# Moving an uneven split from one weight load to a later one, a store to another queue, and regrouping the last stores

## The chip, the cores and the metric

One core of a Trainium2 chip runs the whole kernel. The metric is the device time in microseconds of one execution; several executions are timed and the median counts. All times inside the kernel are counted from the first instruction of the profiled execution.

## The reference

Pooled attention is followed by a soft mixture of experts. There are 8 batches, 8 heads, 576 positions and a head size of 64; the pool is 8; the experts are 8, with 4 slots each (32 slots), a hidden size of 1024 and a model size of 512.

```python
k_p = k.reshape(B, H, Sp, pool, D).mean(axis=3)
v_p = v.reshape(B, H, Sp, pool, D).mean(axis=3)
attn = softmax(scale * q @ k_p.T)               # 576 x 72 for each batch and head
x = (attn @ v_p) as [B * S, H * D]              # 4608 x 512
logits = x @ phi                                # 4608 x 32
slot_input = softmax(logits, axis=0).T @ x      # 32 x 512
for e in range(E):                              # 8 experts, 4 slots each
    slot_out[e] = relu(slot_input[e] @ w1[e]) @ w2[e]
out = softmax(logits, axis=1) @ slot_out        # 4608 x 512, float32
```

All inputs and the output are float32 in HBM. The kernel computes in bf16.

## The kernel before

**Loads.** Nearly everything is read by DMAs that POOL issues, which turn float32 into bf16 on the way. POOL's order is written by hand. It loads `q_sb`, `k_sb` and `v_sb` by pairs of batches (L71, 1152 KB each as bf16), then the eight `w1` matrices (`load_w1`, L78, tile `w_sb`, 1024 KB each), the `w2` of experts 0 to 3 into buffers of the attention (`w_big`, L86), those of experts 4 and 5 into the buffers of qT (`w_qT`, L86), and those of experts 6 and 7 into the buffers of xs (`load_last_w2`, tile `w_xs`, L94 to L98). This text writes w1[e] and w2[e] for the matrices of expert e. In a load of 128 partitions every partition reads one run of HBM: 16 KB for a whole w1 or w2 matrix (8 KB as bf16), 12 KB for the first six of eight rows of w2[6] at L94. At most eight transfers of POOL are in flight: each takes one of eight completion semaphores in turn and waits until the transfer before it on that semaphore has landed.

The load of w1[3] is cut by partitions into three transfers of 112, 8 and 8 partitions; all others have 128.

The last two matrices are loaded in pieces, in this order: w2[6] rows 0 to 5, both column parts (L94); then for each of the two parts of the columns (`PARTS`, 288 on the left and 224 on the right) w2[6] rows 6 and 7 (L96) and w2[7] rows 0 to 5 and 6 and 7 (L98).

**Compute.** Per pair of batches the kernel pools k and v by products with a constant matrix, transposes q, forms scores and exponentials, and the unnormalized `u`, normalizes it into `xs`, and sums up logits and slot inputs. After the last pair the experts' first products (`h_ps`, L432) and the second (`so_ps`, L476, `second`) follow. The order of the end is written out by hand: PE does `second` for experts 0 to 5, eight products on zeros (`warm(8, junk)`), the wide part of w2[6], six products on zeros (`warm(6, junk)`), then for the left and the right column part w2[7], the normalization `slots_out` (DVE, L480), and the output groups.

**Output.** A group of `GROUPS` with n tiles takes n x 128 rows of the output. For each tile PE forms a product `f_ps` (L494), and DVE (L498) or ACT (L496) evicts it by turns with a factor. The first four groups have two tiles and are done for the left and the right columns apart, into `o_sb`; the others have the whole width, into `w_sb`, which reuses the memory of w1. `output` issues the stores (L502) on SP, in the order of the groups; the very first group of each part is stored in two DMAs of 128 rows (`apart`), and in the left part the second group is stored by POOL. Before, the groups from the fifth on have 4, 4, 4, 8 and 8 tiles: three stores of 1 MB, then two of 2 MB.

Of the kernel before, what the change touches and what calls it, by code (L numbers as in the profile page):

```python
# [18 lines left out]
def kernel(  # L19
# [10 lines left out]
    nc = tc.nc  # L30
# [5 lines left out]
    E = moe_w1.shape[0]  # L36
# [11 lines left out]
    DJ = DM // 128  # L48
# [2 lines left out]
    HQ = H // 2  # L51
    NHALF = 4
    PARTS = [slice(0, 9 * DM // 16), slice(9 * DM // 16, DM)]
    GROUPS = [2] * NHALF + [4] * 3 + [8] * 2
    NSPLIT = 2
    NG = 128 // NS

# [15 lines left out]

    w1_sb = persist.tile([128, E, DJ, F], BF)

    def load_w1(e, cuts=()):
        for p0, p1 in zip((0,) + cuts, cuts + (128,)):
            nc.gpsimd.dma_start(out=w1_sb[p0:p1, e],  # L78
                                in_=moe_w1[e, p0 * DJ:p1 * DJ].rearrange("(p j) f -> p j f", j=DJ))

    w2_sb = [None] * E

    def load_w2(experts, pool, tag):
        for e in experts:
            w2_sb[e] = pool.tile([128, FJ, DM], BF, name=f"w2_{tag}", tag=tag)
            nc.gpsimd.dma_start(out=w2_sb[e], in_=moe_w2[e].rearrange("(p j) d -> p j d", j=FJ))  # L86

    def load_last_w2(pool, tag):

        j = FJ - NSPLIT  # L90
        src = [moe_w2[e].rearrange("(p j) d -> p j d", j=FJ) for e in range(E)]
        for e in (E - 2, E - 1):
            w2_sb[e] = pool.tile([128, FJ, DM], BF, name=f"w2_{tag}", tag=tag)
        nc.gpsimd.dma_start(out=w2_sb[E - 2][:, 0:j], in_=src[E - 2][:, 0:j])  # L94
        for cols in PARTS:
            nc.gpsimd.dma_start(out=w2_sb[E - 2][:, j:FJ, cols], in_=src[E - 2][:, j:FJ, cols])  # L96
            for j0, j1 in ((0, FJ - 2), (FJ - 2, FJ)):
                nc.gpsimd.dma_start(out=w2_sb[E - 1][:, j0:j1, cols], in_=src[E - 1][:, j0:j1, cols])  # L98
# [52 lines left out]
    for r in range(2):  # L151
        rows = slice(r * D, (r + 1) * D)
        nc.vector.tensor_copy(out=iphi[rows, :, 0:D],
                              in_=ident[rows, rows].rearrange("p d -> p () d").to_broadcast([D, H, D]))
# [9 lines left out]
    recC = persist.tile([128, 1], FP)  # L164
    recR = persist.tile([128, len(GROUPS), max(GROUPS)], FP)

# [6 lines left out]
    for pair in range(1, NP):  # L173
        for dst, src, name in ((k_sb, k, "k_sb"), (q_sb, q, "q_sb"), (v_sb, v, "v_sb")):
            dst[pair] = load_pair(src, pair, name)
        if pair == NP - 2:
            load_w1(0)

    for e in range(1, E):
        load_w1(e, cuts=(112, 120) if e == 3 else ())  # L180
    load_w2(range(4), big, "big")


# [171 lines left out]
    for pair in range(NP):  # L355
        for qd in range(2):
# [32 lines left out]
            if pair == NP - 1 and qd == 0:  # L389
                load_last_w2(xpool, "xs")  # L390
# [34 lines left out]
    for n in range(E // NG):  # L425
        for half in range(F // 512):
            cols = slice(half * 512, (half + 1) * 512)
            h_ps = ps_m.tile([128, 512], FP, name="h_ps", tag="m")
            for j in range(DJ):
                for g in range(NG):  # L430
                    e = n * NG + g
# [18 lines left out]
    groups = []  # L450
    for n in GROUPS:
        row0 = sum(128 * g[1] for g in groups)
# [4 lines left out]

    R_ps = ps_m.tile([128, len(groups), max(GROUPS)], FP, name="R_ps", tag="m")
    nc.vector.memset(R_ps, 1.0)
# [13 lines left out]
    def second(e, cols, rows=range(FJ)):  # L473
        for fj in rows:
            g = fj % NG
            nc.tensor.matmul(out=so_ps[g * NS:(g + 1) * NS, cols], lhsT=hT[:, e, fj], rhs=w2_sb[e][:, fj, cols],  # L476
                             start=(e == 0 and fj < NG), stop=(e == E - 1 and fj >= NG), skip_group_check=True)

    def slots_out(cols):
        nc.vector.tensor_scalar(out=so[:, cols], in0=so_ps[:, cols], scalar1=recC, scalar2=None, op0=ALU.mult)  # L480

    def output(g, cols, apart=False, queue=nc.sync):

        w = cols.stop - cols.start
        row0, n, rows = groups[g]
        if w == DM:

            e = (row0 // 128 - 2 * NHALF) // 4
            o_sb = w1_sb[:, e:e + n // 4].rearrange("p e j f -> p (e j f)").bitcast(FP).rearrange("p (r c) -> p r c", r=n)
        else:  # L490
            o_sb = opool.tile([128, n, w], FP, name=f"o_sb{w}", bufs=NHALF)
        for r in range(n):
            f_ps = ps_f.tile([128, w], FP, name="f_ps", tag="f")
            nc.tensor.matmul(out=f_ps, lhsT=rows(r), rhs=so[:, cols], start=True, stop=True)  # L494
            if r % 2:
                nc.scalar.activation(out=o_sb[:, r], in_=f_ps, func=AF.Copy, scale=recR[:, g, r:r + 1])  # L496
            else:
                nc.vector.tensor_scalar(out=o_sb[:, r], in0=f_ps, scalar1=recR[:, g, r:r + 1], scalar2=None,  # L498
                                        op0=ALU.mult)
        dst = out[row0:row0 + 128 * n].rearrange("(p r) c -> p r c", r=n)  # L500
        for rs in [slice(r, r + 1) for r in range(n)] if apart else [slice(0, n)]:
            queue.dma_start(out=dst[:, rs, cols], in_=o_sb[:, rs])  # L502


    junk = ps_m.tile([128, 512], FP, name="junk", tag="m")
# [6 lines left out]
    for c in range(2):  # L512
        second(E - 1, PARTS[c])
        slots_out(PARTS[c])
        for g in range(NHALF):

            output(g, PARTS[c], apart=g == 0, queue=nc.gpsimd if (c, g) == (0, 1) else nc.sync)
            if (c, g) == (0, 1):
                second(E - 2, PARTS[1], range(FJ - NSPLIT, FJ))
    for g in range(NHALF, len(groups)):  # L520
        output(g, slice(0, DM))
# [30 lines left out]
```

## Time and profile before

| | before |
|---|---|
| median of 4 runs | 176.53 us (176.51 to 176.63) |
| profiled execution, its own time | 176.63 us |
| its span, first to last instruction | 174.7 us |
| mean granted clock of TensorE | 0.876 |
| busy: PE, DVE, ACT, POOL | 131.5, 94.3, 82.7, 21.4 us |
| moved by POOL's queue (q0) | 30.12 MB, 84.1% of 16 engines' span |
| moved by SP's queue (q1) | 11.50 MB, 16.6% |

In the page's lines of 40 slices, each slice is 4.37 us; the DMA digits are tenths of the 16 DMA engines, and GB/s is what they moved, counted as bf16 where a transfer converts. The chain lists what released what, back from the last instruction: start in us, length in us, engine, tile and line. A line of the windows gives a stretch, its length, the busy time of each engine with the number of its instructions, the granted clock, the DMA share and the GB/s. A line of the timeline gives start and length of one instruction; SPq marks an issue on SP's queue. A line of the DMA issues gives tile and source, issuing queue, how many, the size of each as it is written, and the median time from issue to landing.

### The profile page before, as it was taken

What the parts mean: (1) busy time and instruction counts of PE and PEld (TensorE: products, weight loads), DVE (VectorE), ACT (ScalarE), POOL (GpSimd) and SP (SyncE); (2) the same over time, 40 slices, a digit from 0 to 9 for tenths busy, and PEclk for the clock granted to TensorE, in tenths of its full rate; (3) what the DMA queues carried; (4) which work ended last, traced back from release to release, by engine and by line L of the source; (5) the groups of instructions that cost most, each with busy time, mean ns of one, the idle gap of its engine ahead of it and who ended that gap; (6) DMA issues with size and microseconds to landing.
All of it is one profiled execution on the core that took longest, in us unless ns stands there. A gap on an engine that the chain in (4) does not pass through costs nothing.

```text
span 174.7 us, 3315 instructions
## 1 busy us (share of the span) xinstructions
PE 131.5 (75%) x1357; PEld 80.9 (46%) x1359; DVE 94.3 (54%) x257; ACT 82.7 (47%) x147; POOL 21.4 (12%) x42
## 2 busy tenths in 40 slices
PE   7505799999999999999999975999581198788000
PEld 2304667757866678665754443635440023322000
DVE  2306442677767888778786579543710002899000
ACT  3205459897946988657797540121100001799000
POOL 6000101121000610111130011112111000100000
PEclk9985899999999999999997597599968559999955
DMA  5999999999999999999999999999999999799995
GB/s 188 330 289 218 215 219 211 215 221 213 211 219 221 214 213 219 211 216 216 219 216 212 214 216 216 218 216 218 212 218 214 211 195 161 257 360 416 445 443 244
DMA packets 9518, 41.82 MB, mean 239 GB/s; under 512 B 2128, under 2 KB 5200, under 8 KB 5408
## 3 DMA queue, kind: packets, MB, share of 16 engines
q0 software_dynamic: 6560, 30.12, 84.1%
q1 hardware_dynamic: 2944, 11.50, 16.6%
q8 instruction: 10, 0.16, 0.3%
q14 instruction: 4, 0.03, 0.0%
HBM read 61.93 MB, written 9.44 MB: 409 GB/s over the span
## 4 chain that ended last, share of the span: by engine, by line
DMA 40%; PE 39%; ACT 10%; DVE 2%; issue 1%; SPq 0%; ACTq 0%; DVEq 0%
DMA w_qT<-in_moe_w_dram 20%; DMA q_sb<-in_q_dram 13%; DMA w_sb<-in_k_dram 7%; PE pool_ps L204 7%; PE sc L277 7%; PE u_ps L290 6%; PE q_ps L219 4%; ACT w_sb L496 3%; PE f_ps L494 3%; ACT ex L278 3%; PE G_ps L308 3%; PE junk L125 3%; PE so_ps L476 2%; PE lg_ps L302 1%; ACT vp L269 1%
## 5 line engine op out<-in xcount | busy, mean ns | idle before, releaser
L278 ACT ACTIVATE ex<-sc 72x576 bf16<-72x576 f32 x64 | 39.4, 647 | 14.3 <-PE sc L277 14.0
L296 DVE TENSOR_TENSOR xs<-u_ps,rec 128x384 bf16<-128x384 f32 x72 | 39.4, 552 | 1.6
L290 PE MATMUL u_ps<-vp,ex 72*128 72x97 bf16 (+1 forms) x320 | 27.2, 219 | 2.8 <-DVE xs L296 2.7
L277 PE MATMUL sc<-qT,kp 64*72 64x288 bf16 x128 | 24.5, 313 | 0.8 <-ACT ex L278 0.7
L290 PEld LDWEIGHTS <-ex 72*128 72x128 bf16 (+1 forms) x320 | 17.7, 105 | 12.8 <-issue 4.1
L295 DVE RECIPROCAL rec<-u_ps 128x4 f32<-128x4 f32 x72 | 12.5, 176 | 16.1 <-PE u_ps L290 15.6
L204 PE MATMUL pool_ps<-pmat,k_sb 128*128 128x128 bf16 x144 | 10.9, 232 | 8.3 <-DVE k_sb L169 7.4
L496 ACT ACTIVATE o_sb<-f_ps,recR 128x288 f32<-128x288 f32 (+1 forms) x8 | 3.5, 472 | 25.7 <-PE f_ps L494 25.7
L204 PEld LDWEIGHTS <-k_sb 128*128 128x128 bf16 x144 | 9.4, 104 | 9.2 <-DVE k_sb L169 8.7
L219 PE MATMUL q_ps<-ident,q_sb 128*128 128x128 bf16 x144 | 12.2, 225 | 1.8 <-DMA q_sb<-in_q_dram 0.8
L494 PE MATMUL f_ps<-so,cT 128*128 128x512 bf16 (+2 forms) x44 | 10.8, 339 | 3.2 <-ACT w_sb L496 1.3
L277 PEld LDWEIGHTS <-kp 64*72 64x72 bf16 x128 | 8.6, 108 | 7.7 <-issue 1.5
L225 DVE COPY qT<-q_ps 128x768 bf16<-128x768 bf16 x16 | 8.8, 552 | 5.1 <-PE q_ps L219 4.8
L308 PE MATMUL G_ps<-xs,ee 128*128 128x512 bf16 x36 | 10.9, 444 | 0.4 <-ACT ee L303 0.4
L480 DVE TENSOR_SCALAR so<-so_ps,recC 128x288 bf16<-128x288 f32 (+1 forms) x2 | 1.0, 484 | 18.8 <-PE so_ps L476 18.7
L219 PEld LDWEIGHTS <-q_sb 128*128 128x128 bf16 x144 | 9.1, 100 | 4.0 <-issue 1.5
L125 PE MATMUL junk<-zeros 128*128 128x512 bf16 x25 | 9.7, 548 | 1.4 <-DVE ones L142 1.2
L303 ACT ACTIVATE ee<-lg_ps 128x1152 bf16<-128x1152 f32 (+3 forms) x6 | 4.9, 810 | 12.0 <-PE lg_ps L302 11.9
L498 DVE TENSOR_SCALAR w_sb<-f_ps,recR 128x512 f32<-128x512 f32 x14 | 9.6, 747 | 0.1
L204 PE MATMUL pool_ps<-pmat,v_sb 128*128 128x128 bf16 x144 | 9.6, 219 | 0.0
L496 ACT ACTIVATE w_sb<-f_ps,recR 128x512 f32<-128x512 f32 x14 | 8.9, 684 | 0.9 <-PE f_ps L494 0.3
L204 PEld LDWEIGHTS <-v_sb 128*128 128x128 bf16 x144 | 8.2, 98 | 0.9 <-issue 0.2
(81 smaller groups left out, 151.2 us busy)
## 6 DMA issues: line engine op xcount, KB each, us to landing
w_sb<-in_moe_w_dram POOLq DMA_DIRECT2D x7, 1024.0 KB, 29.3
q_sb<-in_q_dram POOLq DMA_DIRECT2D x4, 1152.0 KB, 15.2
v_sb<-in_v_dram POOLq DMA_DIRECT2D x4, 1152.0 KB, 16.7
w_big<-in_moe_w_dram POOLq DMA_DIRECT2D x4, 1024.0 KB, 31.7
out_dram<-w_sb SPq DMA_DIRECT2D x2, 2048.0 KB, 10.7
k_sb<-in_k_dram POOLq DMA_DIRECT2D x3, 1152.0 KB, 21.6
out_dram<-w_sb SPq DMA_DIRECT2D x3, 1024.0 KB, 6.1
w_qT<-in_moe_w_dram POOLq DMA_DIRECT2D x2, 1024.0 KB, 36.6
```

The source lines that it names most:

```text
L125: nc.tensor.matmul(out=ps, lhsT=zeros[:, 0:128], rhs=zeros, start=True, stop=True)
L204: nc.tensor.matmul(out=ps[:, r].rearrange("p n i -> p (n i)"), lhsT=src[:, tt:tt + 2, :].rearrange("p t d -> p (t d)"), rhs=pmat, start=(t ...
L219: nc.tensor.transpose(out=ps[:, t].rearrange("p n i -> p (n i)"), in_=q_sb[pair][:, tt:tt + 2, :].rearrange("p t d -> p (t d)"), identity= ...
L277: nc.tensor.matmul(out=ps[:, r, 0:S // 2], lhsT=kp[pair][rows, n], rhs=qT[pair][rows, n], start=True, stop=True)
L278: nc.scalar.activation(out=dst.rearrange("p r (i t) -> p r i t", t=NU), in_=ps[:, :, 0:S // 2].rearrange("p r (t i) -> p r i t", i=NI), fu ...
L290: nc.tensor.matmul(out=ps[rows, hh], lhsT=ex[b][:, hh].rearrange("p r t -> p (r t)")[:, c:c + rows.stop - rows.start], rhs=vp[(2 * pair + ...
L295: nc.vector.reciprocal(out=rec, in_=ps[:, :, XW])
L296: nc.vector.tensor_tensor(out=xs[pair][:, t, qd * HQ:(qd + 1) * HQ, :], in0=ps[:, :, 0:XW], in1=rec.rearrange("p h -> p h ()").to_broadcas ...
L308: nc.tensor.matmul(out=ps, lhsT=ee[:, t].rearrange("p g s -> p (g s)"), rhs=x[:, t, :, 0:D], start=(t == 0), stop=(t == 8))
L494: nc.tensor.matmul(out=f_ps, lhsT=rows(r), rhs=so[:, cols], start=True, stop=True)
L496: nc.scalar.activation(out=o_sb[:, r], in_=f_ps, func=AF.Copy, scale=recR[:, g, r:r + 1])
L498: nc.vector.tensor_scalar(out=o_sb[:, r], in0=f_ps, scalar1=recR[:, g, r:r + 1], scalar2=None, op0=ALU.mult)
```

## The change

Three edits go together.

- The split into 112, 8 and 8 partitions is taken from the load of w1[3], which becomes one transfer of 128 partitions, and given to the load of rows 0 to 5 of w2[6] (L94).
- The second left output group is stored by SP, between the first and the third, and no longer by POOL.
- The output groups from the fifth on have 4, 8, 8 and 8 tiles in place of 4, 4, 4, 8 and 8. The 36 tiles, the products and the evictions are the same in number.

```diff
-    GROUPS = [2] * NHALF + [4] * 3 + [8] * 2
+    GROUPS = [2] * NHALF + [4] + [8] * 3
...
-    def load_w1(e, cuts=()):
-        for p0, p1 in zip((0,) + cuts, cuts + (128,)):
-            nc.gpsimd.dma_start(out=w1_sb[p0:p1, e],
-                                in_=moe_w1[e, p0 * DJ:p1 * DJ].rearrange("(p j) f -> p j f", j=DJ))
+    def load_w1(e):
+        nc.gpsimd.dma_start(out=w1_sb[:, e], in_=moe_w1[e].rearrange("(p j) f -> p j f", j=DJ))
...
-        nc.gpsimd.dma_start(out=w2_sb[E - 2][:, 0:j], in_=src[E - 2][:, 0:j])
+
+        for p0, p1 in ((0, 112), (112, 120), (120, 128)):
+            nc.gpsimd.dma_start(out=w2_sb[E - 2][p0:p1, 0:j], in_=src[E - 2][p0:p1, 0:j])
...
-        load_w1(e, cuts=(112, 120) if e == 3 else ())
+        load_w1(e)
...
-    def output(g, cols, apart=False, queue=nc.sync):
+    def output(g, cols, apart=False):
...
-            queue.dma_start(out=dst[:, rs, cols], in_=o_sb[:, rs])
+            nc.sync.dma_start(out=dst[:, rs, cols], in_=o_sb[:, rs])
...
-            output(g, PARTS[c], apart=g == 0, queue=nc.gpsimd if (c, g) == (0, 1) else nc.sync)
+            output(g, PARTS[c], apart=g == 0)
```

The lines of the changed kernel stand one or two higher: L94 stays, L96 and L98 stay, the products of the experts move from L476 to L475, the stores from L502 to L501.

## Prediction

> **What bounds the kernel now.** I read the page's slices first, then the chain of waits in order of time, then windows over the end, then the DMA issues and SP's queue.
>
> ```profile
> DMA  5999999999999999999999999999999999799995
> GB/s 188 330 289 218 215 219 211 215 221 213 211 219 221 214 213 219 211 216 216 219 216 212 214 216 216 218 216 218 212 218 214 211 195 161 257 360 416 445 443 244
> ```
>
> DMA is full in nearly every slice: a load stream to about 149 us (214 GB/s as bf16, read as float32 at twice that), then a store stream. So an edit counts if it changes how soon the last loads land, or how long the DMA engines stand partly idle between loads and stores.
>
> ```profile
> 104.08 34.84 DMA w_qT<-in_moe_w_dram
> 138.91 0.04 issue
> 138.95 1.04 PE so_ps L476 x7
> ...
> 140.76 2.77 PE junk L125 x6
> ...
> 144.42 1.68 PE junk L125 x6
> 146.10 0.57 PE so_ps L476 x8
> ...
> 146.77 0.53 DVE so L480
> ```
>
> The chain leaves DMA at the landing of w2[5] (138.91) and then runs through PE: its products, eight junk products, w2[6], six junk products, w2[7]. Up to 146.10 no load holds it, so the left half of the output starts when w2[5] lands, though later loads are still running.
>
> ```profile
> 149.00:150.00 1.00, 0.63 (x10) 0.21 (x8) 0.94 (x3) 0.71 (x2) 0.69 (x1) 1.00 0.82 282
> 150.00:150.50 0.50, 0.32 (x4) 0.32 (x5) 0.14 (x2) 0.00 (x0) 0.00 (x0) 1.00 0.08 25
> 150.50:151.50 1.00, 0.67 (x6) 0.35 (x4) 1.00 (x3) 0.90 (x3) 0.00 (x0) 1.00 1.00 351
> 151.50:153.50 2.00, 1.55 (x8) 0.63 (x8) 1.87 (x4) 1.75 (x4) 0.00 (x0) 1.00 0.99 330
> 153.50:154.00 0.50, 0.50 (x3) 0.16 (x2) 0.50 (x2) 0.40 (x2) 0.00 (x0) 1.00 0.80 264
> 154.00:155.90 1.90, 1.59 (x6) 0.50 (x5) 1.90 (x4) 1.80 (x4) 0.00 (x0) 1.00 1.02 335
> 155.90:163.70 7.80, 4.69 (x16) 1.70 (x15) 6.01 (x9) 5.68 (x10) 0.00 (x0) 1.00 1.07 440
> ```
>
> The last two columns are DMA share and GB/s. From 150.5 the stores keep the engines full, but for a dip at 153.5 to 154.0. So the end is the start of that full stretch, plus the bytes left, plus any new gap.
>
> ```profile
> 150.97 0.74 SPq L502 DMA_DIRECT2D out_dram<-o_sb  x1
> ...
> 151.76 0.81 SPq L502 DMA_DIRECT2D out_dram<-o_sb  x1
> ...
> 152.68 0.55 SPq L502 DMA_DIRECT2D out_dram<-o_sb  x1
> ```
>
> SP's issues stand nearly end to end from 149.27 to 155.73; the one pause is 150.53 to 150.97, where the first right-hand store waits for its data.
>
> **The change, part by part. (a) The split moves from w1[3] to w2[6].**
>
> ```profile
> w_sb<-in_moe_w_dram POOLq DMA_DIRECT2D x1, 896.0 KB, 31.3
> w_sb<-in_moe_w_dram POOLq DMA_DIRECT2D x2, 64.0 KB, 31.5
> ```
>
> What it does is in the packet records of the trace: each engine ends its part of a transfer with a 4-byte packet, so its progress can be followed. A 16 KB run takes 0.606 us of an engine (packets of 625 ns, overlapping a little). From the end of w1[2] to the end of w1[4] eight engines need 10.38 us (82.79 to 93.17, for one) and eight need 9.16 (83.04 to 92.20): 17 runs against 15. So both 8-row pieces fall on the same eight engines, S; the other eight, N, are relieved by one run. S is put back by 0.606 us, N brought forward by 0.606, and two more closing packets cost each 0.04. The Trainium skill ("DMA: Bandwidth & Descriptors", section "Why a DMA increments its semaphore by 16 and not by 1") lets a copy of 8 partitions run on 8 engines from a cursor that moves on, and names as an exception 16 engines with the partitions rounded up; by the first rule the two pieces would fall on different eights and term (a) would be 0, and 10.38 against 9.16 speaks for the exception.
>
> Engines also fall back one at a time, when an instruction packet (page: q8, 10 packets, 0.3% of 16 engines' span, so some 0.84 us each) lands between their runs. PE's instructions are the same in number, so I keep these where they are. At the end of w2[5] the latest engine is then one of N (closing packet 138.61, an instruction packet ended on it at 131.76); the latest of S are at 138.43 and 138.44. Without the early split N is later by 0.606 - 0.04 = 0.57 and S earlier by 0.65: w2[5] lands at 139.48 instead of 138.91. Then the 12 KB runs (packets of 474 ns, 0.455 apart) give N back 0.455 - 0.04, so from w2[6] on N is 0.15 later than now and S 0.15 earlier: the last load lands at 149.47 instead of 149.32.
>
> On PE the 0.57 enters at 138.95. The granted clock is half until 144.89 in the trace's clock records; PE reaches the second junk block at 144.99 instead of 144.42, now wholly at full clock (0.21 us a product instead of 0.43 for the first), and begins w2[7] at about 146.4 instead of 146.03. The last left products now wait 0.05 us for a load at 146.31 (146.46 after the change), which no longer holds them. Left half: **+0.26**; bounds +0.15 (landing alone) and +0.57 (nothing absorbed), and 0 if the engines do not divide so.
>
> The two extra issues on POOL cost 2 x 0.53 us, near 105 us, with DMA queued over 30 us ahead: nothing. But POOL's waits for a free completion slot (eight in flight) shift by two transfers: the last piece of w2[7], issued at 134.37 after the first w_qT landed, will wait for the 112-row piece of w2[6], about 142.7. Its packets are wanted at about 145.6; from POOL issue to first packet takes 1.25 us (149.27 to 150.5 for POOL's store). 142.7 + 0.1 + 1.25 = 144.1: hidden by 1.5 us.
>
> Small pieces cost little in this trace: the two of 64 KB land 0.73 and 0.59 us behind the first (89.21, 89.94, 90.53), about one run each, and the later transfers follow at the old pace. A rule of the same page speaks against them: it gives each DMA about 2.0 us fixed ("Anatomy of one DMA — SWDGE (gpsimd) path"), so two more on the path would be an estimated 4 us, and the sum near 181.
>
> **(b) The second left store goes from POOL to SP.** Its data is ready at 148.72; POOL wakes late (149.27, first packet 150.5). On SP it goes out at 149.17 and the engines resume up to 0.1 us sooner. Behind it the two other left stores, then all right-hand ones, move back by its 0.61 us and 0.1 between issues, 0.71, less the pause of 0.44: 0.27, and with the left half 0.26 late (the right-hand data is ready by then) the first right-hand issue comes at 151.56 instead of 150.97. Whether that reaches the end depends on the 0.74 and 0.81: left-hand stores of the same 128-row shape took 0.35 and 0.43. If the excess is back-pressure (some 40 runs an engine are queued then), SP catches up 0.4 to 0.8 us, DMA stays full and the dip at 153.5 even shrinks: -0.15. If they always take that long, the fourth right-hand store finds the engines empty: +0.33. The window 151.50:153.50 (0.99) says DMA, not SP, sets the pace there, so I take a value nearer the lower end: **+0.1**.
>
> **(c) Two stores of 1 MB become one of 2 MB.** Per engine 16 packets of 315.8 ns become 8 of 615.9: 5.05 against 4.93 us, **-0.11** (bounds -0.13 and 0). The larger store waits for twelve evicted tiles, 156.54 now, some 156.8 then; first packet by 157.9, while the 1 MB store ahead keeps the engines until about 158.9. That cover hides the wait; without it 1.2 us (156.54 less 155.39) would show. Evictions and PE's products are the same in number.
>
> Sum: 0.26 + 0.1 - 0.11 = +0.25 us. The profiled execution is 176.63 (span 174.7 and 1.9 around it), 0.10 above the median of 176.53; against the median the forecast is 176.8.
>
> **The rivals.** Slower: SP becomes the bound. Mechanism: 0.74 and 0.81 belong to the right-hand 128-row stores, every later issue is 0.59 late, and DMA runs dry before the fourth right-hand store. It decides once that store's issue is later than some 152.8. For it: there is a dip at 153.5 already. Against it: the window of 0.99. Price 0.59 - 0.11 = +0.48: 177.0.
>
> Faster: unloading S matters more than loading N, because the instruction packets fall elsewhere; w2[5] then lands no later, the last load 0.15 sooner, and with POOL's late wake-up gone and the larger store: -0.15 - 0.1 - 0.11, 176.2. Against it: the second instruction packets, at 122.0 and 130.8, sit on engines of N.
>
> Nothing in the split: eight-row pieces of a 12 KB row spread evenly, or PE's full clock absorbs all: +0.1 - 0.11, 176.5.
>
> Late issue: the last piece of w2[7] starts after 145.6 and the stream runs dry; about 1 us: 177.6.
>
> **How the numbers follow.** Main forecast 0.40, SP bound 0.34, faster 0.10, nothing in the split 0.12, late issue 0.04. Some 0.2% (0.35 us) is what can be told from no change here. Beyond 176.88: SP bound, late issue, and a little of the main forecast above its value: 0.42. Below 176.18: about half of the faster case and the ends of two others: 0.10. Rest 0.48. Range: from 176.2 (the faster case) to 177.3 (SP bound with 0.3 of the landing not absorbed).
>
> **What would show it.** The landing of w2[5] near 139.5 and the first products on it as late; the last load near 149.5; left so at 147.0; ten o_sb issues on SP; the window before the fourth right-hand store full or with a new dip; w_sb stores without a dip between them. Wrong if w2[5] lands no later than 139.0, if the last piece of w2[7] lands after 150, or if DMA's share falls below 0.9 after 156.

## The result and the profile after

The changed kernel takes 176.78 us (median of 41 runs, 176.65 to 177.13) and the kernel before 176.55 (61 runs, 176.45 to 176.77). The ratio is 1.0013, 95% interval 1.0009 to 1.0018: 0.23 us slower, which lies within the 0.2% that the prediction had named. 176.8 was forecast.

The profiled execution of the changed kernel took 176.67 us with a span of 174.57. The span of before was 174.70 in 176.63. So in these two executions the span became *shorter*, and the time around it grew from 1.93 to 2.10 us. The medians say the same: less the mean time around the span (1.91 before, 2.11 after), they are 174.64 and 174.67 us. Nearly all of the 0.23 us lies outside the span, where the prediction had no term.

The 40 slices of the changed kernel (DMA in tenths, GB/s) show the same two streams:

```profile
DMA  5999999999999999999999999999999999799995
GB/s 195 329 280 222 215 215 213 222 213 215 218 210 219 218 213 219 213 220 216 214 212 222 210 218 218 212 216 216 214 216 220 208 191 163 249 356 420 454 439 248
```

The chain of waits of the changed kernel, in order of time (start, length, what):

```profile
129.74 16.61 DMA w_xs<-in_moe_w_dram
146.36 0.04 issue
146.40 0.31 PE so_ps L475 x2
...
146.81 0.53 DVE so L479
```

and PE's timeline between the landing of w2[5] and the left half of the output:

```profile
139.47 1.04 PE L475 MATMUL so_ps<-w_qT,hT 128*32 128x512 bf16 x8 [3.71 <-DMA w_qT<-in_moe_w_dram]
...
144.25 1.47 PE L125 MATMUL junk<-zeros 128*128 128x512 bf16 x6
145.71 0.42 PE L475 MATMUL so_ps<-w_xs,hT 128*32 128x288 bf16 x6
146.40 0.30 PE L475 MATMUL so_ps<-w_xs,hT 128*32 128x288 bf16 x2 [0.27 <-DMA w_xs<-in_moe_w_dram]
```

PE starts on w2[5] at 139.47 instead of 138.95, as forecast. But the chain no longer leaves DMA there: PE reached w2[7] at 145.71, before its last rows had landed (146.36), and waited for them. The granted clock had gone back to full at 143.4 in this execution (144.9 in the one of before), and that made up the delay. The left half then starts at 146.81, only 0.04 late.

The windows over the end, as in the prediction (the last two columns are DMA share and GB/s):

```profile
150.00:150.50 0.50, 0.26 (x3) 0.27 (x4) 0.18 (x1) 0.00 (x0) 0.00 (x0) 1.00 0.19 62
150.50:151.50 1.00, 0.67 (x7) 0.35 (x5) 0.95 (x3) 0.84 (x3) 0.00 (x0) 1.00 0.98 335
151.50:153.50 2.00, 1.55 (x7) 0.69 (x7) 1.87 (x4) 1.75 (x4) 0.00 (x0) 1.00 1.01 342
153.50:154.00 0.50, 0.50 (x3) 0.23 (x2) 0.50 (x2) 0.40 (x2) 0.00 (x0) 1.00 0.84 276
154.00:155.90 1.90, 1.65 (x6) 0.57 (x6) 1.90 (x4) 1.80 (x4) 0.00 (x0) 1.00 1.04 346
155.90:163.70 7.80, 4.68 (x16) 1.70 (x15) 6.07 (x9) 5.73 (x10) 0.00 (x0) 1.00 1.04 435
```

From 150.5 on they carry the same load as before. The dip at 153.5 is as large as it was (0.84, before 0.80), and no gap shows in the window that holds 158.5, where the first 2 MB store takes over (1.04). On SP the stores of the right half follow without a pause, and the two that had taken 0.74 and 0.81 us take less:

```profile
151.25 0.61 SPq L501 DMA_DIRECT2D out_dram<-o_sb  x1
...
151.96 0.58 SPq L501 DMA_DIRECT2D out_dram<-o_sb  x1
...
152.64 0.55 SPq L501 DMA_DIRECT2D out_dram<-o_sb  x1
```

The late issue that the prediction had weighed is there, and hidden, in POOL's timeline:

```profile
139.72 0.84 POOL L98 DMA_DIRECT2D w_xs<-in_moe_w_dram  x1 [4.04 <-DMA w_qT<-in_moe_w_dram]
142.97 0.70 POOL L98 DMA_DIRECT2D w_xs<-in_moe_w_dram  x1 [2.42 <-DMA w_xs<-in_moe_w_dram]
```

The last piece of w2[7] is issued at 142.97 instead of 134.37 and still lands at 149.38 (before: 149.32).

### The profile page after: what moved, and what is told of

It reads as the page before. It is cut to its first block, busy times and chain, and to the rows that moved or that the text cites. A ratio compares the mean times of both kernels' runs of the same rounds, so it can differ in the third digit from the quotient of the medians.

```text
span 174.6 us, 3310 instructions
## 1 busy us (share of the span) xinstructions
PE 135.1 (77%) x1357; PEld 83.0 (48%) x1359; DVE 94.2 (54%) x257; ACT 82.9 (47%) x147; POOL 20.8 (12%) x41
## 4 chain that ended last, share of the span: by engine, by line
DMA 56%; PE 24%; ACT 8%; DVE 1%; issue 1%; POOL 1%; SPq 0%; POOLq 0%; ACTq 0%; DVEq 0%
DMA w_big<-in_moe_w_dram 22%; DMA w_sb<-in_moe_w_dram 17%; DMA w_xs<-in_moe_w_dram 10%; DMA w_sb<-in_k_dram 7%; PE pool_ps L203 6%; PE q_ps L218 5%; PE sc L276 4%; PE f_ps L493 3%; ACT w_sb L495 3%; PE u_ps L289 2%; ACT ex L277 1%; ACT vp L268 1%; ACT o_sb L495 1%; PE fold_ps L229 1%; PE G_ps L307 1%
## 5 line engine op out<-in xcount | busy, mean ns | idle before, releaser
L218 PE MATMUL q_ps<-ident,q_sb 128*128 128x128 bf16 x144 | 13.5, 242 | 0.4 <-ACT kpar L206 0.3
L218 PEld LDWEIGHTS <-q_sb 128*128 128x128 bf16 x144 | 10.2, 109 | 2.6 <-issue 1.2
L203 PE MATMUL pool_ps<-pmat,v_sb 128*128 128x128 bf16 x144 | 10.3, 228 | 0.0
L203 PEld LDWEIGHTS <-v_sb 128*128 128x128 bf16 x144 | 8.9, 103 | 1.0 <-issue 0.2
```

What stands on the lines that cost most here:

```text
L203: nc.tensor.matmul(out=ps[:, r].rearrange("p n i -> p (n i)"), lhsT=src[:, tt:tt + 2, :].rearrange("p t d -> p (t d)"), rhs=pmat, start=(t ...
L218: nc.tensor.transpose(out=ps[:, t].rearrange("p n i -> p (n i)"), in_=q_sb[pair][:, tt:tt + 2, :].rearrange("p t d -> p (t d)"), identity= ...
```

## The experiments

In each, "before" is the kernel before, run on the same chip beside it. "Outside" is an execution's time less its span, a mean over the runs.

| run | edit | median, before beside it | ratio and interval | outside | w2[5] lands | left so | last store lands |
|---|---|---|---|---|---|---|---|
| before | | 176.55 | 1 | 1.91 | 138.91 | 146.77 | 173.79 |
| changed | (a) split, (b) store, (c) groups | 176.78, 176.55 | 1.0013 (1.0009 to 1.0018) | 2.11 | 139.43 | 146.81 | 173.65 |
| e1 | (a) | 176.98, 176.58 | 1.0023 (1.0013 to 1.0034) | 2.11 | 139.41 | 146.83 | 173.84 |
| e2 | (b) | 176.94, 176.58 | 1.0024 (1.0015 to 1.0033) | 1.91 | 138.85 | 146.70 | 173.65 |
| e3 | (c) | 176.53, 176.58 | 0.9999 (0.9990 to 1.0008) | 1.91 | 138.84 | 146.68 | 173.62 |
| e4 | (b), (c) | 176.44, 176.58 | 0.9994 (0.9985 to 1.0003) | 1.92 | 138.89 | 146.74 | 173.58 |
| e5 | (b), (c), no split | 177.62, 176.57 | 1.0057 (1.0044 to 1.0070) | 2.11 | 139.56 | 147.40 | 174.23 |
| e6 | changed, fewer junk products | 176.73, 176.57 | 1.0006 (0.9997 to 1.0014) | 2.11 | 139.49 | 146.91 | 173.75 |
| e7 | (b), (c), both splits | 176.89, 176.57 | 1.0021 (1.0011 to 1.0031) | 1.90 | 138.90 | 147.22 | 174.05 |
| e8 | (b), (c), split at w1[7] | 176.65, 176.57 | 1.0005 (0.9996 to 1.0013) | 2.12 | 138.80 | 146.66 | 173.51 |
| e9 | changed, one ACT instruction more | 176.69, 176.64 | 1.0004 (0.9995 to 1.0014) | 1.90 | 139.44 | 146.83 | 173.68 |
| e10 | changed, one DVE instruction more | 176.83, 176.64 | 1.0010 (1.0001 to 1.0019) | 2.11 | 139.55 | 146.95 | 173.81 |
| e11 | e8, one ACT instruction more | 176.42, 176.61 | 0.9991 (0.9982 to 1.0000) | 1.91 | 139.09 | 146.90 | 173.74 |
| e12 | changed, more junk products | 176.83, 176.61 | 1.0023 (1.0010 to 1.0036) | 2.11 | 139.50 | 146.89 | 173.74 |

"Left so" is the start of the left half's normalization (`slots_out`). "Outside" is read from spans given to 0.1 us. The last three columns are those of one profiled execution each.

### e1: the split alone

```diff
-        nc.gpsimd.dma_start(out=w2_sb[E - 2][:, 0:j], in_=src[E - 2][:, 0:j])
+        for p0, p1 in ((0, 112), (112, 120), (120, 128)):
+            nc.gpsimd.dma_start(out=w2_sb[E - 2][p0:p1, 0:j], in_=src[E - 2][p0:p1, 0:j])
...
-        load_w1(e, cuts=(112, 120) if e == 3 else ())
+        load_w1(e)
```

> The kernel before with the moved split alone (w1[3] whole, rows 0 to 5 of w2[6] in 112, 8 and 8 partitions). Theory A, the split is what slows: the landing of w2[5] near 139.45 instead of 138.91, the last load within 0.2 us of 149.32, and the median 0.15 to 0.40 above the kernel before, with a wider scatter, since PE must then make up the 0.55 us and does so only where its granted clock returns to full before some 144 us. Rival B, the split is neutral because the last load alone sets the start of the stores: within 0.08 of before, and the whole difference of the change comes from the store or from the time outside the span.

Measured: 0.40 us slower, the upper end of theory A; w2[5] at 139.41, the last load at 149.38. Rival B falls. But 0.19 of the 0.40 lies outside the span, which theory A had no place for. The other 0.2 lies in the spans (174.8 to 175.1; before 174.6 to 174.8); the profiled execution, with 174.75, is one of the shortest, and its left half is only 0.06 late.

### e2: the store alone

```diff
-            output(g, PARTS[c], apart=g == 0, queue=nc.gpsimd if (c, g) == (0, 1) else nc.sync)
+            output(g, PARTS[c], apart=g == 0, queue=nc.sync)
```

> The kernel before with the second left store on SP alone. Theory A: SP's longer queue is hidden, since DMA is full; first w_sb store issued within 0.1 of 154.74, median -0.15 to +0.05 against before. Rival B, the time outside the span (2.1 us in the changed kernel, 1.93 before) comes with this edit: span shorter by 0.1, median 0.05 to 0.15 above. Rival C, SP is the bound: first w_sb store 0.25 or more later, median +0.2 to +0.35.

Measured: 0.36 us slower, and for none of the reasons given. The first w_sb store is issued at 154.59, 0.15 sooner than before, and the last store lands at 173.65, 0.14 sooner, though 0.07 of that is an earlier left half in this execution. The loss stands behind it. The waits of SP at the kernel's end in e2 (who waited for what: us in total, times, longest):

```profile
SPq L547 <- DMA out_dram<-w_sb: 11.3, 1, 11.3
```

and the same waits of before:

```profile
SPq L547 <- DMA out_dram<-w_sb: 11.0, 3, 4.8
```

At the end SP polls (waits on, one after the other) the eight completion semaphores of its queue, in an order that is the same in all these kernels. Before, the last store has the eighth of them: SP waits for the last three stores in turn, and one poll follows on the last landing. One store more on SP shifts the last store to the first semaphore: SP waits 11.3 us there, and then has the other seven still to pass, 0.06 us each. From the last landing to the end of the span it takes 1.34 us instead of 0.91. That 0.43, less the 0.14 won, is the 0.28 by which this execution's span is longer than that of before; the medians differ by 0.36.

### e3: the groups alone

```diff
-    GROUPS = [2] * NHALF + [4] * 3 + [8] * 2
+    GROUPS = [2] * NHALF + [4] + [8] * 3
```

> The kernel before with groups of 4, 8, 8 and 8 tiles alone. Theory A: 16 packets of 316 ns an engine become 8 of 616, median -0.05 to -0.13. Rival: the later issue of the first 2 MB store (156.5 instead of 155.4) opens a gap in the stores near 158.5: median +0.1 or more.

Measured: -0.05 us, an interval that holds no change. The last store lands 0.17 sooner, of which 0.09 is an earlier left half in that execution; the rest, 0.08, is what the larger packets gain. One store fewer on SP puts the last one on the seventh semaphore, which leaves one poll more, 0.06. No gap opened: the 2 MB store is issued at 156.47, the 1 MB store ahead of it lands at 158.91.

### e4: store and groups

> The changed kernel with the split left at w1[3]: the store on SP and the new groups, no split at w2[6]. Theory A: w2[5] lands at 138.9 again, the scatter is that of the kernel before, and the median is 0.1 to 0.25 below before (faster than both). Rival B (the store or the groups cost the time): median 0.1 to 0.25 above before, as the changed kernel.

The edits are those of e2 and e3. Measured: 0.14 us below before, with an interval that still holds 1, and 0.34 below the changed kernel. With one store more and one fewer the last store is back on the eighth semaphore, the end takes 0.92 us, and what is left is the gain of both. So the two edits are not additive: +0.36 and -0.05 give -0.14. The chain of e4's profile leaves DMA not at w2[5], as in the one of before, but at w2[7] (146.29), with the clock at full from 142.75; its left half starts at 146.74, 0.03 sooner. The rest of the changed kernel is the split: 0.23 + 0.14 = 0.37 us, of which 0.19 lies outside the span.

### e5, e7 and e8: where a split stands

The edits of e5 and e8 are shown against e4.

```diff
-        load_w1(e, cuts=(112, 120) if e == 3 else ())
+        load_w1(e)
```

> The store on SP and the new groups, and no split anywhere. Theory A (every split relieves eight engines N by one run and loads eight engines S with one): w2[5] lands at 139.4 as in the changed kernel, and the last load 0.4 us later still than with the split at w2[6], near 149.75; median 176.8 to 177.2. Rival: the split only costs, and without it the last load lands by 149.3. The time outside the span (1.92 us in four kernels, 2.10 in the two with the moved split) is open: 1.92 if the split rows of w2[6] cost it, 2.10 if the missing split of w1[3] does.

e7 keeps the cut of w1[3] and cuts w2[6] too, so its edit is that w1[3]'s call is left as before:

```diff
-        load_w1(e)
+        load_w1(e, cuts=(112, 120) if e == 3 else ())
```

> The store on SP and the new groups, and both splits, at w1[3] and at w2[6]. Theory A: w2[5] lands at 138.9 as before; after w2[6] the engines S are 0.46 later and N 0.46 earlier, so the last load is one of S, at 149.3 - 0.18 + 0.5 = 149.6; median 0.2 to 0.35 above the kernel with the split at w1[3] alone (176.44), if the time outside is 1.92, and 0.2 more if it is 2.10. Rival, two splits even the engines out better: the last load sooner than 149.2.

```diff
-        load_w1(e, cuts=(112, 120) if e == 3 else ())
+        load_w1(e, cuts=(112, 120) if e == 7 else ())
```

> The store on SP and the new groups, with the split at w1[7] instead of w1[3]. Theory A: where it stands among the early loads makes no difference: w2[5] at 138.9, last load at 149.3, time outside the span 1.92, median 176.4 to 176.5. Rival, the place of the split decides by itself (the later the worse): median above 176.6.

Measured, against e4: without a split w2[5] lands 0.67 later and the last load at 149.93 (e4: 149.30); with both, w2[5] at 138.90 and the last load at 149.72; with the split at w1[7], 138.80 and 149.21. All three go the way of theory A's two groups of engines: one split levels them, none leaves N late, two make S late. In e5 and e7 the last loads were 0.18 and 0.12 later than worked out. Where the early split stands makes no difference to the loads (e8), and its span of 174.42 us is the shortest of the profiled ones. Outside the span, though, e8 is at 2.12, as are the other kernels so far with w1[3] whole; that, and not the place of the split, puts its median over 176.6, where the rival had it. e5 has a further loss that I had not expected: its end takes 1.31 us from the last landing (e4: 0.92), for POOL takes 0.42 us instead of 0.08 over the first of the barriers at which the engines wait for one another. POOL's program has two instructions fewer in e5; whether that is the reason was not tried, and the cause is open.

### e6 and e12: how much PE has to spare

```diff
-    warm(8, junk)
+    warm(5, junk)
```

> The changed kernel with five instead of eight junk products after the products of w2[5] (nothing of the result uses them). Theory A, PE carries the late landing of w2[5] to the left half whenever its clock is still half: with 1.3 us less at half clock it never does; the slow end of the scatter (177.0 to 177.1) goes, and the median falls by 0.05 to 0.2, to 176.6 to 176.75. Rival: the scatter comes from the loads or the stores: no change.

e12 goes the other way:

```diff
-    warm(8, junk)
+    warm(11, junk)
```

> The changed kernel with eleven instead of eight junk products after the products of w2[5]. Theory A, PE from the landing of w2[5] on has 0 to 0.4 us to spare before the left half: three more products of 0.21 to 0.43 us put the left half 0.3 to 1.2 us later, median 177.2 to 177.9 with a wide scatter by the clock. Rival, loads alone set the left half: median within 0.1 of the changed kernel.

Measured: e6 176.60 to 176.88 in 12 runs, the changed kernel 177.0 or more in 5 of 41. In e6's profiled execution the clock was half until 145.3. Its chain leaves DMA at the third piece of w2[6] (143.03), after which PE runs on at half clock:

```profile
114.35 28.69 DMA w_xs<-in_moe_w_dram
143.03 0.14 issue
...
144.14 2.02 PE junk L125 x6
146.16 0.65 PE so_ps L475 x8
```

The left half starts at 146.91; by the load of w2[7] (146.45, and 0.45 from there to the left half as in the changed kernel's chain) it could start at 146.90. So w2[5] no longer sets it, as theory A has it, but PE and the loads are level here too. 12 runs without one above 177 could be chance: the slow runs of the changed kernel go with the granted clock (its five runs at 0.857 and 0.858 have spans of 174.9 to 175.0), and no run of e6 had that clock. Nor are such runs the split's alone: e4, e8 and e11, where w2[5] lands at 138.80 to 139.09, have one run each at 0.857, with a span of 175.0, while the runs of before at 0.857 and 0.858 have 174.6 to 174.8. No trace caught a slow one.

e12 hardly moved the median (176.83), against the expected 177.2 to 177.9; but 3 of 10 runs took 177.2 to 177.8. Its profiled execution, one of the others, shows how they escape: the clock is back at full at 143.15, so the last of the nine junk products take 0.21 us each, and the chain, now through PE, is as late as the load would make it.

```profile
141.34 3.00 PE junk L125 x9
...
144.82 1.47 PE junk L125 x6
146.29 0.50 PE so_ps L475 x8
```

So in these profiles PE's path and the loads are level to about 0.1 us, and the clock decides which one ends last. With the clock full by about 143 PE has more to spare than I had put.

### e9 and e10: the time outside the span

```diff
     nc.scalar.activation(out=dummy, in_=zeros[:, 0:1], func=AF.Exp)
+    nc.scalar.activation(out=dummy, in_=zeros[:, 0:1], func=AF.Exp)
```

> The changed kernel with one more tiny ACT instruction at the start (the dummy exponential twice), in ACT's idle time. Six kernels with w1[3] whole have 185 instructions on ACT and 273 on DVE and spend 2.10 to 2.12 us outside the span; five with w1[3] cut have 186 and 274 and spend 1.91 to 1.93. Theory D, the length of ACT's program sets it: 1.92 outside, median 0.19 lower, 176.6. Theory E, that of DVE's: 2.10 outside, median 176.78. Theory F, it is the transfers themselves: 2.10.

e10 repeats an instruction of DVE instead:

```diff
     nc.vector.memset(ones[:, 0:1], 1.0)
+    nc.vector.memset(ones[:, 0:1], 1.0)
```

> The changed kernel with one more tiny DVE instruction (a memset of one column twice). Theory E, the length of DVE's program sets the time outside the span: 1.92, median 176.6. Theory D (ACT's) and theory F (the transfers): 2.10, median 176.78.

(The kernels with w1[3] whole were five then, not six.) Measured: with one more instruction on ACT the time outside is 1.90 us in ten runs (1.88 to 1.95), with one more on DVE 2.11 (2.05 to 2.15). Theory D holds, E and F fall. The link to w1[3] is this: a cut w1[3] is three loads. Those ACT evictions that overwrite its memory then wait for three completions instead of one, which takes one wait instruction more: ACT has 184 instructions in the traces instead of 183 (the expectation counts two more in each). Without the cut it is one shorter, and the execution 0.2 us longer around the span. Only these two lengths were tried, and why the one costs more, no run shows.

e10's profile also caught the case that the prediction had worked out, with the clock half until 144.87. Its chain:

```profile
104.06 35.49 DMA w_qT<-in_moe_w_dram
139.55 0.04 issue
139.60 1.05 PE so_ps L476 x7
140.64 3.53 PE junk L125 x8
144.17 0.79 PE so_ps L476 x5
...
145.00 1.47 PE junk L125 x6
146.47 0.39 PE so_ps L476 x8
```

Here the chain leaves DMA at w2[5], the second junk block starts at 145.00 and the left half at 146.95, 0.18 later than in the profile of before.

### e11: a version ahead of both

```diff
-        load_w1(e, cuts=(112, 120) if e == 3 else ())
+        load_w1(e, cuts=(112, 120) if e == 7 else ())
...
     nc.scalar.activation(out=dummy, in_=zeros[:, 0:1], func=AF.Exp)
+    nc.scalar.activation(out=dummy, in_=zeros[:, 0:1], func=AF.Exp)
```

> The store on SP, the new groups, the split at w1[7], and one more tiny ACT instruction. If the length of ACT's program alone sets the time outside the span, it is 1.91 instead of 2.11 and the median 0.2 under that of the split at w1[7] without it: 176.4 to 176.5, below both kernels. Rival, the 0.2 goes with the cut of w1[3]: 2.11 and 176.65 again.

Measured: 176.42 (before 176.61), outside 1.91. The same kernel without the idle ACT instruction, e8, took 176.65. It is 0.1% faster than before with an interval that ends at 1.0000, and is level with e4 (176.44), which needs nothing but (b) and (c).

## Why the prediction was right, and where not

**The sum** was +0.25; +0.23 was measured. The measured parts are (a) +0.37, of which some 0.18 in the span and 0.19 outside, and (b) with (c) -0.14. The forecast parts were +0.26, +0.1 and -0.11, all in the span; there the change is worth only 0.03 to 0.04. So the number came out right by luck: the terms in the span were together some 0.2 too high, and a term that was not in the sum made it up. I count the mechanism of the loads as confirmed, not the sizes.

**(a), the engines.** The step from packet records to two groups of engines was right: w2[5] at 139.48 forecast, 139.43 measured; the last load at 149.47 forecast, 149.38 measured. The packet records of the changed kernel show the other side of it: from the end of w1[2] to the end of w1[4], with w1[3] whole, the engines no longer fall into eights of 10.38 and 9.16 us; nearly all need some 9.73. e5 and e7 move the last load the way that the step says. The Trainium skill's exception in "DMA: Bandwidth & Descriptors" (section "Why a DMA increments its semaphore by 16 and not by 1"), 16 engines with partitions rounded up for some SWDGE copies (those that POOL issues), agrees with these landings; its general rule, a cursor that moves on, would have left e5 and e7 alike.

**(a), PE.** The mis-sized step is the one on the clock: +0.26 for the left half, which was to start at 147.0 and starts at 146.81 in the profile. I took the half clock to last until 144.89, as in the one trace. It ends at 143.4 in the profile of the changed kernel, where the loads set the left half and 0.04 us is lost; in e10 it ends at 144.87 and 0.18 is lost against the forecast 0.26 (PE starts w2[7] at 146.40, as forecast, but its products then follow without a stall). The 0.26 does not follow from its own figures either: 146.4 less 146.03, less the 0.05 of waiting, is 0.32. How much of the 0.18 in the span is this term stays open: with three junk products fewer (e6) the median fell by only 0.05, and the changed kernel's longest spans have their like in kernels without the moved split.

**(a), what was left out.** The time around the span was taken as fixed at 1.9 us. It grew by 0.19 to 0.20, with one instruction fewer on ACT (e9, e11), and that is most of the measured difference.

**(b)** had bounds of -0.15 and +0.33 and I took +0.1. The last store landed 0.14 sooner in e2, of which 0.07 is the earlier left half, so the stores gained some 0.07 (the lower bound was 0.15): the excess of 0.74 and 0.81 was not a property of these stores, since in the changed kernel the same two take 0.61 and 0.58. The first right-hand issue came at 151.25; the 151.56 of the prediction is 151.50 by its own terms. The rival in which SP becomes the bound falls with it: the first w_sb store went out at 154.70 instead of 154.74. What no step held is the end of SP's program. Alone, the edit costs 0.36; (c) takes that back.

**(c)** was about right: -0.11 forecast, and -0.05 in e3 (its interval also holds no change), whose last store sits one semaphore earlier.

**The late issue** stayed hidden: 142.97 against the forecast 142.8, with the last load not disturbed.

## What to carry to other kernels

When a stream of transfers ends a stage, look at the engines one by one: here a piece of eight rows loaded half of them, and its worth depends on which half is late at the time when somebody waits, not only at the end. Test edits to a queue together and apart: one store more on a queue can cost more at the final waits than it wins in the stream, and another edit can cancel it. At a quarter of a microsecond, compare the span and the time around it separately before explaining either.

## What was not expected of the hardware

- One instruction on ACT changes the time outside the span by 0.2 us: 1.90 to 1.92 us in the seven kernels with 184 instructions on ACT in the trace (before, e2, e3, e4, e7, e9, e11), 2.11 to 2.12 in the seven with 183.
- The order of the final polls matters: some 0.06 us for each semaphore that comes after the last store's, 0.43 us in all in e2 with seven of them.
- Two 8-row pieces of 48 KB land 0.16 us apart behind their 112-row piece (142.69, 142.85, 143.01); the fixed 2.0 us a DMA of the Trainium skill's page "DMA: Bandwidth & Descriptors" (section "Anatomy of one DMA — SWDGE (gpsimd) path") does not show in transfers queued behind one another.
